# Column sums of an attention kernel: one fold by an accumulating DMA, the last half folded like the others

## The chip, the cores and the metric

The kernel runs on one core of a Trainium2 chip. The metric is the time of one execution on the device, in microseconds; the time of the kernel before is 1118.45 us, the median of three runs (1118.39 to 1118.84).

## The reference

Pooled attention, followed by a mixture of experts in which each token goes to one expert. All inputs are float32. The change lies in the attention, in the denominator of the softmax.

```python
# q, k, v: (8 batches, 8 heads, 1152 rows, 64)
q_pool = q.reshape(B, H, S // 2, 2, D).mean(axis=3)           # 576 queries
scores = (1.0 / np.sqrt(D)) * np.matmul(q_pool, k.transpose(0, 1, 3, 2))
scores = scores - np.max(scores, axis=-1, keepdims=True)
attn = np.exp(scores)
attn = attn / (np.sum(attn, axis=-1, keepdims=True) + 1e-09)
attn_out = np.matmul(attn, v)
x = attn_out.transpose(0, 2, 1, 3).reshape(4608, 512)         # tokens
# logits = x @ w_gate; each token to its argmax expert (of 8):
# out = gate_weight * (relu(x_e @ w1[e]) @ w2[e])
```

## The kernel before, in words

**Tiling.** The attention takes the eight batches one after the other, in each of them four pairs of heads (`hp` 0 to 3), in each pair two halves of the 576 pooled queries (`half` 0 and 1; `HQ` = 288 queries). One half of one pair is a unit; there are 64. A unit's scores stand in a tile `s` of 128 partitions x 9 chunks x 2 heads x 288, keys along the partitions. `scores` (from line 618 on) has TensorE form the products of a chunk into PSUM (`st`, line 640), VectorE take them into `s` with a running minimum (line 644), and ScalarE raise the whole to the exponential in place, two chunks at a time (line 675). `values` multiplies the exponentials with the values (`pa`, line 779).

**The column sums.** The denominators are sums over keys, that is over the nine chunks and the 128 partitions. `chunk_sum` makes them. GpSimd first folds the nine chunks of a unit to two: `fold` = chunks 0 to 2 plus chunks 3 to 5 (the first fold, 1728 numbers in a partition), plus chunks 6 to 8 (the second), then its third chunk onto its first (the third fold, 576 numbers); all three are on line 735. For a whole pair TensorE then multiplies both units' folded tiles with a matrix of ones, in four column strips of the array (`total`, line 725), and ScalarE or VectorE adds the result to `sm`. Two cases differ. The last pair of the last batch goes to TensorE unfolded (`whole`, line 718). And the second half of the last pair of every other batch is folded half way: GpSimd does the first fold alone (line 731), TensorE sums the three folded chunks and the three raw ones itself (line 718).

**What sets the order.** Every piece of work is recorded in a `Flow` with its engine, an estimate of its time, a key, the steps it needs and the tiles it holds; `emit` then walks through a plan in which each engine takes the ready step of the least key, and writes the instructions down in that order. So another piece of work in one place can move the instructions of every engine. On the chip each engine works through its own queue in order and waits by semaphores. Of `s` there are four buffers, of `fold` three. GpSimd also adds the two rows of each pooled query (`qp` from `qn`, line 529), and issues the scatters of the routing's lists (`lists`, line 960) of the batch before, six to a batch. SP issues the loads of `kp`, `qn` and `vn` (line 499).

**After the attention** the expert layers follow (lines 1363 and 1393), with weights `raw` loaded through SP and tokens gathered by GpSimd.

## Time and profile before

| what | value |
|---|---|
| median of three runs | 1118.45 us |
| the profiled execution: its time, its span | 1113.62 us, 1111.7 us |
| granted TensorE clock, mean | 0.999 of full speed |
| TensorE busy, share of the span | 1100.8 us, 99% |
| VectorE | 875.5 us, 79% |
| GpSimd | 854.2 us, 77% |
| ScalarE | 624.2 us, 56% |

The profile is of one execution; its span runs from the first to the last instruction, and its own time has a little around that. The attention ends at some 655 us of the span. PE is TensorE, DVE VectorE, ACT ScalarE, POOL GpSimd, SP the engine that issues most loads. A time in a timeline is counted from the span's start. The share of busy time is a mean over the whole program, so the views by stretch and by engine say more than the table. A matmul's record has a length of its own while the next one already runs, so the pace of TensorE is read from start to start; a float32 product stands in the profile as two records for each instruction of the order.

### The profile page before, as it was taken

To read this page: it belongs to the slowest core of one execution; us is meant where nothing else is said; L and a number is where in the kernel's file an instruction comes from. 1 tells how busy PE (TensorE), PEld (TensorE's weight loads), DVE (VectorE), ACT (ScalarE), POOL (GpSimd) and SP (SyncE) were. 2 spreads that over 40 slices of the span, in tenths; PEclk is the share of its full clock that TensorE was granted. 3 is DMA by queue.
4 is the path that set the end of the run, shared out by engine and by line. 5 is a ranking of instruction groups with operands and counts; after the bars stand their busy time and mean duration, and the time that the engine had idled before them with its cause. 6 is when DMAs were issued, how large, how long until landed. Compare 5 with 4: busy or idle time off the path is not lost.

```text
span 1111.7 us, 32995 instructions
## 1 busy us (share of the span) xinstructions
PE 1100.8 (99%) x13317; PEld 793.8 (71%) x13317; DVE 875.5 (79%) x2244; ACT 624.2 (56%) x835; POOL 854.2 (77%) x488
## 2 busy tenths in 40 slices
PE   9999999999999999999999999999999999999997
PEld 5555556565655565665665568999888989899896
DVE  7988988989989989989999959755555556677761
ACT  4656666566565666557655564444444444555561
POOL 3999999999999999999999943766666655555511
PEclk9999999999999999999999999999999999999999
DMA  9976747738648558558545069865555566677640
GB/s 159 167 120 111 128 76 123 129 66 125 115 73 139 97 85 141 94 89 146 81 84 107 3 227 212 244 180 176 176 169 167 184 195 191 194 248 252 224 159 30
DMA packets 387502, 158.06 MB, mean 142 GB/s; under 512 B 302694, under 2 KB 357762, under 8 KB 387342
## 3 DMA queue, kind: packets, MB, share of 16 engines
q1 hardware_dynamic: 376718, 134.91, 55.7%
q0 software_dynamic: 10464, 20.78, 5.8%
q8 instruction: 106, 1.74, 0.7%
q14 instruction: 54, 0.44, 0.2%
q10 hardware_dynamic: 160, 0.20, 0.1%
HBM read 135.02 MB, written 22.07 MB: 141 GB/s over the span
## 4 chain that ended last, share of the span: by engine, by line
PE 87%; issue 7%; POOL 4%; DVE 1%; DMA 1%; POOLq 0%; ACT 0%
PE st L640 24%; PE pa L779 24%; PE ph L1363 16%; PE py L1393 16%; PE st L725 3%; POOL fold L735 2%; PE st L718 1%; DVE s L644 1%; POOL xr L1092 1%; PE st L856 1%; PE st L665 1%; POOL out_dram L1402 1%; POOL xq L1092 1%; PE st L801 0%; DMA xr<-x_runs,ix 0%
## 5 line engine op out<-in xcount | busy, mean ns | idle before, releaser
L675 ACT ACTIVATE s<-s,bias 128x1152 f32<-128x1152 f32 (+1 forms) x320 | 346.7, 1149 | 172.5 <-DVE bias L671 172.4
L644 DVE TENSOR_SCALAR_CACHE_REDUCE s<-st 128x576 f32<-128x576 f32 x576 | 416.1, 746 | 30.3 <-PE st L640 28.1
L640 PE MATMUL st<-qT,kT 64*64 64x288 f32 x4608 | 363.6, 406 | 1.5 <-DVE s L644 0.9
L779 PE MATMUL pa<-s,vn 64*64 64x288 f32 x4608 | 358.5, 403 | 0.3 <-DVE xT L786 0.3
L640 PEld LDWEIGHTS st<-qT,kT 64*64 64x64 f32 x4608 | 167.4, 133 | 115.3 <-DVE s L644 22.4
L779 PEld LDWEIGHTS pa<-s,vn 64*64 64x64 f32 x4608 | 172.2, 133 | 98.4 <-DVE xT L786 3.5
L735 POOL TENSOR_TENSOR fold<-s 128x1728 f32<-128x1728 f32 x55 | 212.9, 3870 | 4.6 <-ACT s L675 4.4
L735 POOL TENSOR_TENSOR fold<-fold,s 128x1728 f32<-128x1728 f32 x55 | 213.4, 3879 | 0.5
L1363 PE MATMUL ph<-xh,w1h 128*128 128x248 f32 (+4 forms) x512 | 155.8, 304 | 0.6 <-DVE hl L1373 0.6
L1363 PE MATMUL ph<-xl,w1h 128*128 128x248 f32 (+4 forms) x512 | 154.6, 302 | 0.0
L1363 PE MATMUL ph<-xh,w1l 128*128 128x248 f32 (+4 forms) x512 | 154.6, 302 | 0.0
L1235 DVE TENSOR_TENSOR w2l<-raw,w2h 128x1024 fp32r<-128x1024 f32 x64 | 78.3, 1223 | 85.0 <-ACT w2h L1320 81.3
L1092 POOL DMA_INDIRECT xr<-x_runs,ix x76 | 96.8, 1274 | 51.8 <-issue 23.9
L1393 PE MATMUL py<-w2h,hh 128*128 128x512 f32 x328 | 128.1, 391 | 0.0
L1393 PE MATMUL py<-w2l,hh 128*128 128x512 f32 x328 | 127.8, 390 | 0.0
L1393 PE MATMUL py<-w2h,hl 128*128 128x512 f32 x328 | 127.8, 390 | 0.0
L1402 POOL DMA_INDIRECT out_dram<-y,rec x41 | 44.0, 1073 | 90.0 <-ACT y L1410 73.1
L1371 ACT ACTIVATE hh<-ph 128x372 fp32r<-128x372 f32 (+4 forms) x100 | 49.3, 493 | 106.5 <-PE ph L1363 106.4
L1363 PEld LDWEIGHTS ph<-xh,w1h 128*128 128x128 f32 x512 | 96.4, 188 | 3.4 <-DVE hl L1373 1.5
L1363 PEld LDWEIGHTS ph<-xl,w1h 128*128 128x128 f32 x512 | 96.5, 188 | 0.8
L1363 PEld LDWEIGHTS ph<-xh,w1l 128*128 128x128 f32 x512 | 96.5, 188 | 0.0
L1373 DVE SCALAR_TENSOR_TENSOR hl<-ph,hh 128x372 fp32r<-128x372 f32 (+4 forms) x100 | 55.6, 556 | 48.6 <-ACT hh L1371 48.5
(230 smaller groups left out, 1339.0 us busy)
## 6 DMA issues: line engine op xcount, KB each, us to landing
raw<-in_moe_w_dram SPq DMA_DIRECT2D x128, 512.0 KB
kp<-in_k_dram SPq DMA_DIRECT2D x124, 144.0 KB
vn<-in_v_dram SPq DMA_DIRECT2D x124, 144.0 KB
qn<-in_q_dram SPq DMA_DIRECT2D x120, 144.0 KB
x_runs<-row SPq DMA_DIRECT2D x96, 99.0 KB
xr<-x_runs,ix POOLq DMA_INDIRECT x76, 4.7
x_runs<-empty SPq DMA_DIRECT2D x4, 297.0 KB
xq<-x_runs,ix POOLq DMA_INDIRECT x52, 2.9
```

The lines of the kernel that those rows point to most:

```text
L640: nc.tensor.matmul(pt.t[to, h, :HQ], x.kT.t[up, c * P + i * D:c * P + (i + 1) * D], x.qT.t[up, cols], start=True, stop=True, tile_position ...
L644: nc.vector.tensor_scalar(s.t[:, c], pt.t[:, :, :HQ], -SCALE, None, op0=ALU.mult, op1=ALU.min, accum_out=mx.t[:, c:c + 1],)
L675: nc.scalar.activation(s.t[:, c0:c0 + n], s.t[:, c0:c0 + n], AF.Exp, bias=bias.t, scale=-1.0)
L735: add = lambda to, a, b: nc.gpsimd.tensor_tensor(to, a, b, ALU.add)
L779: mark.made = nc.tensor.matmul(pa.t[cs, i, :HQ], x.vn.t[up, h, c, :], s.t[up, c, h], start=c == 0, stop=c == NC - 1, tile_position=(up.sta ...
L1092: ins = nc.gpsimd.indirect_dma_start(out=x.xr[i // NQD].t[:, i % NQD, :], out_offset=None, in_=xg, in_offset=bass.IndirectOffsetOnAxis(ap= ...
L1235: (nc.gpsimd if eng == "POOL" else nc.vector).tensor_tensor(lo, raw, hi.bitcast(F32), ALU.subtract)
L1363: mark.made = nc.tensor.matmul(view()[:, i, :], a[:, c, fp], b[:, c, :n], start=c == 0 and k == 0, stop=c == NDC - 1 and k == 2)
L1371: a = f.add("ACT", act(nb * n) - 44, lambda home=home, apart=apart: nc.scalar.activation(home(0), apart(), AF.Relu), at - 20, done(p), [ph ...
L1373: d = f.add("DVE", dve(nb * n), lambda home=home, apart=apart: nc.vector.scalar_tensor_tensor(home(1), apart(), 0.0, home(0).bitcast(F32), ...
L1393: mark.made = nc.tensor.matmul(py.t, blocks(a)[:, c * x.nr + r], b[:, c % 2, :], start=c == 0 and k == 0, stop=c == NFC - 1 and k == 2)
L1402: ins = nc.gpsimd.indirect_dma_start(out=out, out_offset=bass.IndirectOffsetOnAxis(ap=x.re.t.bitcast(I32)[:, r, 0:1], axis=0), in_=y.t, in ...
```

## The change

The half-way case is gone: the second half of a batch's last pair is folded three times by GpSimd like the others, and `total` sums it. And in the first half of the first and the third pair (`hp` 0 and 2) of every batch but the last, the second fold is no longer an addition by GpSimd. GpSimd issues a DMA that reads chunks 6 to 8 of `s` and adds them to `fold` where it lies (`accum_op=ALU.add`, 884,736 B); the third fold waits for its landing. For the plan it stands as 1100 ns on GpSimd and 4700 ns on the DMA. `one` is false throughout, so the lines under it do nothing.

```diff
-        on_pe = by_units or not o.exact and hp == NHP - 1 and half == 1
+        on_pe = by_units
...
+        one = not o.exact and (False)
...
-        half_way = on_pe and not by_units
-        if half_way:
-            u = tile_of(o, "fold", [P, 3, 2, HQ], bufs=FOLD_BUFS, pool=o.rt)
-            p = f.add("POOL", pool(6 * HQ), lambda: nc.gpsimd.tensor_tensor(u.t, s.t[:, 0:3], s.t[:, 3:6], ALU.add),
-                      key, every(ready[:6]), [s, u])
-        elif not on_pe:
+        if not on_pe:
...
             p = f.add("POOL", pool(6 * HQ), lambda: add(u.t, s.t[:, 0:3], s.t[:, 3:6]), key, every(ready[:6]), [s, u])
-            p = f.add("POOL", pool(6 * HQ), lambda: add(u.t, u.t, s.t[:, 6:9]), key, done(p, *every(ready[6:])), [s, u])
+            if not o.exact and (half == 0 and b < B - 1 and hp % 2 == 0):
+                p = f.add("POOL", 1100, lambda: nc.gpsimd.dma_start(out=u.t, in_=s.t[:, 6:9], accum_op=ALU.add), key, done(p, *every(ready[6:])), [s, u])
+                p = f.add("DMA", 4700, lambda: None, key, done(p), [s, u], late=800)
+            else:
+                p = f.add("POOL", pool(6 * HQ), lambda: add(u.t, u.t, s.t[:, 6:9]), key, done(p, *every(ready[6:])), [s, u])
             p = f.add("POOL", pool(2 * HQ), lambda: add(u.t[:, 0], u.t[:, 0], u.t[:, 2]), key + R_FOLD3, done(p), [u])
...
-        if half_way:
-            parts.append(lambda: whole(ps, begin, [*(u.t[:, c] for c in range(3)), *(s.t[:, c] for c in range(6, NC))]))
-            needs, holds, ns = [*needs, *done(p), *every(ready[6:])], [*holds, s, u], ns + 485 * 3
-        elif on_pe:
+        if on_pe:
```

The change moves instructions. On GpSimd, around the last half of batch 3 and the first half of batch 4, the order before is this (the fold made of `s_4568` is the half-way one, the one of `s_4690` is batch 4's first):

```order
L735 TENSOR_TENSOR fold_4723<-fold_4723,s_4433 128x1728
L529 TENSOR_TENSOR qp_4840<-qn_4331 128x576
L731 TENSOR_TENSOR fold_4858<-s_4568 128x1728
L735 TENSOR_TENSOR fold_4723<-fold_4723 128x576
L735 TENSOR_TENSOR fold_4932<-s_4690 128x1728
L529 TENSOR_TENSOR qp_4990<-qn_4860 128x576
L735 TENSOR_TENSOR fold_4932<-fold_4932,s_4690 128x1728
L735 TENSOR_TENSOR fold_4932<-fold_4932 128x576
```

In the change, at the same place (`s_4539` is the last half, `s_4672` batch 4's first):

```order
L529 TENSOR_TENSOR qp_4816<-qn_4499 128x576
L732 TENSOR_TENSOR fold_4834<-s_4539 128x1728
L732 TENSOR_TENSOR fold_4697<-fold_4697 128x576
L732 TENSOR_TENSOR fold_4834<-fold_4834,s_4539 128x1728
L732 TENSOR_TENSOR fold_4963<-s_4672 128x1728
L732 TENSOR_TENSOR fold_4834<-fold_4834 128x576
L735 DMA fold_4963<-s_4672 128x1728
L529 TENSOR_TENSOR qp_5044<-qn_4838 128x576
L732 TENSOR_TENSOR fold_5066<-s_4796 128x1728
L732 TENSOR_TENSOR fold_5066<-fold_5066,s_4796 128x1728
L732 TENSOR_TENSOR fold_4963<-fold_4963 128x576
```

The last half has three folds now, the next unit's first fold among them, and its third fold is the fifth from its first on. Behind the issue of the transfer come the pooling of queries and two folds of the other half, and only then the third fold that needs its landing.

On GpSimd, in the third pair of batch 4, first half, where the lists' scatters of batch 3 stand, before:

```order
L735 TENSOR_TENSOR fold_5597<-s_5283 128x1728
L960 DMA lists<-re_5124,di_5441 42240x2
L735 TENSOR_TENSOR fold_5597<-fold_5597,s_5283 128x1728
L960 DMA lists<-re_5124,di_5441 42240x2
L735 TENSOR_TENSOR fold_5738<-s_5485 128x1728
L960 DMA lists<-re_5124,di_5441 42240x2
L735 TENSOR_TENSOR fold_5738<-fold_5738,s_5485 128x1728
L960 DMA lists<-re_5124,di_5441 42240x2
L735 TENSOR_TENSOR fold_5597<-fold_5597 128x576
```

In the change:

```order
L732 TENSOR_TENSOR fold_5558<-s_5252 128x1728
L960 DMA lists<-re_5112,di_5411 42240x2
L735 DMA fold_5558<-s_5252 128x1728
L529 TENSOR_TENSOR qp_5636<-qn_5381 128x576
L960 DMA lists<-re_5112,di_5411 42240x2
L732 TENSOR_TENSOR fold_5702<-s_5459 128x1728
L960 DMA lists<-re_5112,di_5411 42240x2
L732 TENSOR_TENSOR fold_5702<-fold_5702,s_5459 128x1728
L960 DMA lists<-re_5112,di_5411 42240x2
L732 TENSOR_TENSOR fold_5558<-fold_5558 128x576
```

The second fold `fold<-fold,s` of that half has become the DMA. The pooling of queries has moved behind it, and three scatters and two folds stand between the transfer's issue and the third fold.

On TensorE, the sum of batch 3's last pair, before:

```order
L640 MATMUL st_5040<-qT_4870,kT_4721 64x288 x4
L779 MATMUL pa_4947<-s_4568,vn_4222 64x288 x4
L725 MATMUL st_5057<-fold_4723,ones_73 32x288 x4
L718 MATMUL st_5057<-fold_4858,ones_73 32x288 x6
L718 MATMUL st_5057<-s_4568,ones_73 32x288 x6
L640 MATMUL st_5083<-qT_4870,kT_4721 64x288 x4
L779 MATMUL pa_5091<-s_4690,vn_4552 64x288 x4
```

In the change:

```order
L640 MATMUL st_5027<-qT_4836,kT_4705 64x288 x4
L640 MATMUL st_5037<-qT_4836,kT_4705 64x288 x4
L727 MATMUL st_5046<-fold_4697,ones_73 32x288 x4
L727 MATMUL st_5046<-fold_4834,ones_73 32x288 x4
L779 MATMUL pa_5061<-s_4672,vn_4532 64x288 x4
L665 MATMUL st_5074<-ident,top 64x64 x4
```

Of the sixteen matmuls of the sum eight are left, and those of the last half read its folded tile alone.

## Rows read from the trace of the kernel before

**Rows 1.** The page, part 1: busy us (share of the span) xinstructions.

```profile
PE 1100.8 (99%) x13317; PEld 793.8 (71%) x13317; DVE 875.5 (79%) x2244; ACT 624.2 (56%) x835; POOL 854.2 (77%) x488
```

**Rows 2.** Busy us by stretch (PE, PEld, DVE, ACT, POOL), clock, DMA share, GB/s.

```profile
400.00:500.00 100.00, 100.00 (x1672) 60.57 (x1668) 91.47 (x271) 62.15 (x78) 98.38 (x40) 1.00 0.62 102
```

**Rows 3.** GpSimd's timeline: start us, us, line, operation [idle before <-releaser].

```profile
366.73 3.86 POOL L735 TENSOR_TENSOR fold<-s 128x1728 f32<-128x1728 f32 x1 [0.71 <-ACT s L675]
...
411.12 3.90 POOL L731 TENSOR_TENSOR fold<-s 128x1728 f32<-128x1728 f32 x1
...
446.80 3.86 POOL L735 TENSOR_TENSOR fold<-s 128x1728 f32<-128x1728 f32 x1 [0.35 <-ACT s L675]
...
459.49 3.87 POOL L735 TENSOR_TENSOR fold<-s 128x1728 f32<-128x1728 f32 x1
...
464.47 3.87 POOL L735 TENSOR_TENSOR fold<-fold,s 128x1728 f32<-128x1728 f32 x1
...
480.80 3.89 POOL L735 TENSOR_TENSOR fold<-s 128x1728 f32<-128x1728 f32 x1
484.64 1.41 POOL L735 TENSOR_TENSOR fold<-fold 128x576 f32<-128x576 f32 x1
486.01 3.85 POOL L735 TENSOR_TENSOR fold<-fold,s 128x1728 f32<-128x1728 f32 x1
489.83 1.40 POOL L529 TENSOR_TENSOR qp<-qn 128x576 f32<-128x576 f32 x1
491.19 3.88 POOL L731 TENSOR_TENSOR fold<-s 128x1728 f32<-128x1728 f32 x1
```

**Rows 4.** The waits of GpSimd, 100 to 600 us: us in total, times, longest.

```profile
POOL fold L735 <- ACT s L675: 1.4, 3, 0.7
```

**Rows 5.** TensorE's timeline, batch 1, the sum of the third pair.

```profile
166.21 0.69 PE L725 MATMUL st<-fold,ones 128*32 128x288 f32 x8 [0.47 <-POOL fold L735]
```

**Rows 6.** TensorE's timeline in batch 5: the third pair's sum, then the last pair's.

```profile
486.46 1.18 PE L725 MATMUL st<-fold,ones 128*32 128x288 f32 x16
487.56 0.71 PE L779 MATMUL pa<-s,vn 64*64 64x288 f32 x8
...
504.45 0.69 PE L725 MATMUL st<-fold,ones 128*32 128x288 f32 x8
...
506.53 0.71 PE L640 MATMUL st<-qT,kT 64*64 64x288 f32 x8
```

**Rows 7.** DMA issues on GpSimd: lines 960 and 1056, the gathers' group, landing.

```profile
L960 POOL DMA_INDIRECT lists<-re,di x48: 915/922/1710, 130.7 to 684.6; - x48
...
DMA to landing us min/median/max: 3.4/5.1/6.1
...
L1056 POOL DMA_DIRECT2D li<-lists x13: 687/728/741, 695.7 to 930.7; - x13
...
L1092 POOL DMA_INDIRECT xr<-x_runs,ix x76 | 96.8, 1274 | 51.8 <-issue 23.9
```

**Rows 8.** Timelines, GpSimd and TensorE: the start, batch 0, batch 6.

```profile
22.50 3.89 POOL L735 TENSOR_TENSOR fold<-s 128x1728 f32<-128x1728 f32 x1 [2.25 <-ACT s L675]
...
31.94 1.41 POOL L529 TENSOR_TENSOR qp<-qn 128x576 f32<-128x576 f32 x1 [1.60 <-DMA qn<-in_q_dram]
...
91.62 3.87 POOL L731 TENSOR_TENSOR fold<-s 128x1728 f32<-128x1728 f32 x1
...
102.53 0.69 PE L725 MATMUL st<-fold,ones 128*32 128x288 f32 x8
...
584.52 0.69 PE L725 MATMUL st<-fold,ones 128*32 128x288 f32 x8
```

**Rows 9.** The page, part 3: packets, MB, share of 16 engines.

```profile
q0 software_dynamic: 10464, 20.78, 5.8%
```

**Rows 10.** VectorE's timeline, the second pair's queries turned.

```profile
38.66 0.47 DVE L542 STREAM_TRANSPOSE qT<-qp 128x288 f32<-128x288 f32 x1
```

**Rows 11.** DMA share in tenths, 40 slices, 420 to 500 us.

```profile
DMA  4599998775984799951750006949500006406999
```

More of the change, by code (lines that the diff above doesn't have):

```diff
@@ L736, in chunk_sum @@
             p = f.add("POOL", pool(6 * HQ), lambda: add(u.t, s.t[:, 0:3], s.t[:, 3:6]), key, every(ready[:6]), [s, u])
-            p = f.add("POOL", pool(6 * HQ), lambda: add(u.t, u.t, s.t[:, 6:9]), key, done(p, *every(ready[6:])), [s, u])
+            if not o.exact and (half == 0 and b < B - 1 and hp % 2 == 0):
[3 more added lines that the diff above has]
+                p = f.add("POOL", pool(6 * HQ), lambda: add(u.t, u.t, s.t[:, 6:9]), key, done(p, *every(ready[6:])), [s, u])
             p = f.add("POOL", pool(2 * HQ), lambda: add(u.t[:, 0], u.t[:, 0], u.t[:, 2]), key + R_FOLD3, done(p), [u])
+            if one:
+                p = f.add("POOL", pool(2 * HQ), lambda: add(u.t[:, 0], u.t[:, 0], u.t[:, 1]), key, done(p), [u])
             if half == 0:
@@ L748, in chunk_sum @@
             parts.append(lambda: total(ps, v, 0, True))
-            needs, holds, ns = done(q), [ps, v], 485
+            needs, holds, ns = done(q), [ps, v], 0 if one else 485
         begin = not parts
-        if half_way:
-            parts.append(lambda: whole(ps, begin, [*(u.t[:, c] for c in range(3)), *(s.t[:, c] for c in range(6, NC))]))
-            needs, holds, ns = [*needs, *done(p), *every(ready[6:])], [*holds, s, u], ns + 485 * 3
-        elif on_pe:
+        if on_pe:
             parts.append(lambda: whole(ps, begin, [s.t[:, c] for c in range(NC)]))
```

## The prediction, made before the changed kernel ran

> **What bounds the kernel now.** The page's busy line comes first: TensorE is busy for 99% of the span, GpSimd for 77% [rows 1]. A mean over stages with different limits says little, so next the busy time by stretch: in 100 us of the attention TensorE has 100.0 and GpSimd 98.4 [rows 2]. The reader is to see that two engines are full there, not one. Which of them sets the pace is read from GpSimd's timeline and its waits. From one of its waits for ScalarE to the next it works without a hole: it waits 0.71 us before the fold at 366.73 and 0.35 us before the one at 446.80 [rows 3], so one batch of its work takes 446.80 - 0.35 - 366.73 = 79.72 us. A batch itself takes 80.07 us (the half-way folds of two batches start at 411.12 and 491.19 [rows 3]). So TensorE sets the pace and GpSimd has 0.35 us to spare per batch; over 500 us it waits for work for 1.4 us in all [rows 4]. Early on it is the other way round: in batch 1 TensorE stands for 0.47 us in the middle of a sum, until a fold is done [rows 5]. A change that relieves one engine gains only until the other one holds it, and that is the whole question here.
>
> **TensorE's part.** The sum of a batch's last pair issues 32 records before (8 for the first half, 24 for the three half-summed and the three raw chunks), 16 after. The short form is there already: 486.46 to the next product at 487.56 is 1.10 us; the long one is 504.45 to 506.53, 2.08 us [rows 6]. Seven such sums save 0.98 us each, **6.9 us** in all, 80.07 - 0.98 = 79.09 us per batch. The order shows as many changes between the two ways of splitting the array as before, so nothing more comes off.
>
> **GpSimd's part, per batch.** From start to start [rows 3] a first fold takes 3.84 us (480.80 to 484.64), a third 1.37 (to 486.01), a second 3.82 (to 489.83), the pooling of a pair's queries 1.36 (to 491.19). Removed: two second folds, 7.64 us. Added: a second and a third fold for the batch's last half, 5.19 us, and two issues of a transfer. No accumulating transfer is in the trace. Below, its issue is bounded by the direct transfer of 128 rows, 0.73 us; above by the gathers, 1.27 us. The nearest indirect one, the scatter of the lists, takes 0.92 [rows 7], and with the gaps around it 1.14 us (459.49 to 464.47 less a fold [rows 3]). So an issue with its gap of 0.2 occupies 0.93 to 1.47 us; I take 1.05, between the direct one and the scatter, because it is direct but reads two places for each it writes. Net: -7.64 + 5.19 + 2.10 = -0.35 us, which makes **79.37 us** per batch (79.1 to 80.2). That is more than TensorE's 79.09: by these rows GpSimd takes over the pace.
>
> **Where the chain is tied.** The last half's sum now waits for five folds instead of one: its first fold, the third of the half before, its second, the next unit's first, its third, as the order shows, 3.84 + 1.37 + 3.82 + 3.84 + 1.37 = 14.24 us. Before, the sum of batch 0 stood 102.53 - 91.62 = 10.91 us behind that fold's start [rows 8], and waited for none of it. In batch 0 the transfer of the third pair lets GpSimd start it 3.82 - 1.05 = 2.77 us earlier, at 88.85, so the five end at 103.1. That of the first pair brings nothing: GpSimd then waits until 31.94 for queries anyway [rows 8]. From there six batches at 79.37 give 579.3 for the same sum in batch 6, which stood at 584.52 [rows 8]: 5.2 us earlier, and the sum itself is 0.98 shorter, **-6.2 us**. The last batch's work is as before.
>
> **What the transfers cost beside that.** (1) The first one is issued when the first fold of 22.50 is done, at 26.4, and flies while the next pair's queries come in, for which GpSimd already waits until 31.94 [rows 8]. Both source and target have to be read; 884,736 B at the mean rate of GpSimd's queue, 20.78 MB in 5.8% of 16 engines' 1111.7 us = 20.1 KB/us each, 322 in all [rows 9], are 2.75 us, twice that is 5.5. If its data flow from 27.5 on, the queries are held up for the 4.4 us until 31.94 at half their rate, 2.2 us; if only from 32 on, not at all. GpSimd's chain starts later by as much, TensorE's not, which wants these queries turned at 38.66 [rows 10]. I take **+1.0**, the middle. (2) Landing: the scatter, about 1 KB, lands 5.1 us after its issue [rows 7]. With 2.75 to 5.5 us of data the transfer lands after 7.9 to 10.6 us. In the first pair the order puts the queries' pooling and two folds between issue and third fold, 1.05 + 1.36 + 3.84 + 3.82 = 10.1 us of cover; in the third pair three scatters more, 13.5 us. So the wait at the first pair's third fold is 0 to 0.5 us; with 0.2 and six of them **+1.2**. The rule in the Trainium skill, "DMA: Bandwidth & Descriptors" (Anatomy of one DMA), gives an estimate of 2.0 us plus the bytes over 436 KB/us: 4.0 us, with no wait at all, and the sum would be 1.2 us lower. That the scatter takes 5.1 us for 1 KB speaks against it here. (3) Loads: a transfer can hold loads up by its 5.5 us. The cover is that the list of 500 us of GpSimd's waits names no load, ScalarE alone in more than the gaps of issues [rows 4]; without it the next query sum would wait that long. (4) The scores of a half are held until the landing instead of the second fold's end. They are overwritten four units later, 40 us, so that costs nothing.
>
> **Sum:** -6.2 + 1.0 + 1.2 = -4.0 us against the profiled execution's 1113.62 us (span 1111.7): 1109.6. The median of the runs shown, 1118.45, lies 4.83 above that execution, so the forecast is **1114.4 us**.
>
> **Rivals.**
> - *TensorE keeps the pace.* If the issue is at its low end and all landings are early, TensorE's 6.9 us and the 0.47 us that it waited [rows 5] come off: 1111.1. For it: the direct issue's 0.73 us. Against it: the five folds ahead of the last half's sum. Chance 0.10.
> - *Nothing is left.* An issue as long as a gather's, 1.27 plus a gap of 0.2, is 0.42 us more at 13 transfers (one in batch 0, two in each of six): -4.0 + 5.5 = +1.5, 1119.9, inside 0.2% (2.2 us, about what a measurement here can tell from no change). For it: the second read. Against: it is direct. Chance 0.17.
> - *Slower: the transfer lands after its cover.* Place: the third fold of the first pair's first half, which stands in GpSimd's queue; behind it are the next unit's first fold and everything else, and TensorE waits for that pair's sum. Each us of wait in six batches takes 6 us from the 5.2 that are left without landings; at 0.9 us nothing is left, at 1.25 it is slower by 0.2%, so it decides from a landing 11.3 us after the issue. With 2 us the time is 1118.45 - 5.2 + 12 = 1125.3. For it: load bursts fill the engines, 90% in many slices of a batch [rows 11], and a transfer that gets half of them needs 5.1 + 5.5 to 11 us. Against: the mean share is 62% [rows 2], and several slices in a row are idle [rows 11]. Chance 0.18.
> - *Slower: the issue itself is held up.* The longest scatter took 1.71 us against 0.92 [rows 7]; if each issue cost that and a gap, 1.9, 13 times 0.85 us more is +11.1: 1125.5. Against: 0.92 is median and nearly the least, beside a VectorE that is 91% busy [rows 2, 7]. Such a rule stands in the Trainium skill, "SBUF — State Buffer" (Who interferes with whom): GpSimd cannot write descriptors while VectorE runs in a mode that takes the port they share. By that rule the issue would stretch; these rows don't show it. Chance 0.04.
>
> **Numbers.** The forecast's own case has 0.51 and holds 1112 to 1116.5. Faster by over 0.2% are nearly all of it, the first rival and a little of the second: 0.58. Within 0.2%: the second and the edge of the late landing, 0.20. Slower: 0.22. The range goes from the first rival, 1111, to 1122, where the late landing means waits of 1.5 us; some 0.1 lies above it.
>
> **What would show it.** TensorE's records at the last pair's sum fall from 32 to 16, its busy time by some 6 us and a batch to 79.3 to 79.5 us. GpSimd's page line stands near 850 us, with 14 transfers of about 1.0 us, landing 8 to 10.6 us after issue; TensorE's waits for folds grow, at the batch's last sums. The forecast is wrong if a batch takes 79.1 us (TensorE), or 80 us and more with GpSimd waiting for a transfer ahead of third folds (late landing) or without such waits (dear issue), or if the first queries come more than 2 us later.

## The result, and the profile after

The changed kernel takes **1124.91 us** (median of seven runs, 1119.02 to 1129.78) where the kernel before takes 1118.45 (seven runs, 1117.55 to 1121.32): a ratio of 1.0052, with a 95% interval of 1.0031 to 1.0072. It is slower by half a per cent; forecast were 1114.4 us, faster by 0.36%. Timed again later, the same kernel came out at 1.0015 (0.999 to 1.004), 1.0004 (0.9995 to 1.0013) and 1.0003 (0.9993 to 1.0013). Here and below a ratio leaves out the few executions that ran in a slow state and the medians do not, so a ratio need not be that of two medians. So there are two questions: what eats the forecast gain everywhere, and what cost half a per cent more the first time.

The profiled execution took 1124.91 us, its span is 1123.3. The page's busy line and GpSimd's DMA queue, which answer to [rows 1, 9]:

```profile
PE 1101.2 (98%) x13205; PEld 810.6 (72%) x13205; DVE 878.6 (78%) x2244; ACT 622.8 (55%) x835; POOL 845.3 (75%) x502
...
q0 software_dynamic: 12480, 33.16, 12.1%
```

GpSimd is busy for 8.9 us less, but 5.3 of these lie in the gathers of the expert layers, which the change leaves alone (96.8 us before, 91.5 here). TensorE's busy time did not fall by the 6 us of the forecast in this execution. In a later pair of profiles on one chip (set 5 below) both come out as forecast: TensorE 1097.3 in place of 1102.5, GpSimd 851.1 in place of 855.2. The transfers, by their line (min/median/max ns of the issue on GpSimd):

```profile
L735 POOL DMA_DIRECT2D fold<-s x14: 839/978/1146, 27.7 to 550.2; - x14
```

The queue's 12.38 MB more are the 14 transfers; their data are 128 packets of 6912 B each, of 542 ns at the median and 623 at the mean. The first packet of a transfer begins 1.4 to 2.4 us after the issue (5.1 once), and the last one ends 6.7 to 9.2 us after it (11.4 the same once). GpSimd's waits from 100 to 570 us, beside [rows 4], name no landing of a transfer; the four largest are:

```profile
POOL lists L960 <- issue: 4.0, 24, 0.2
POOL fold L732 <- issue: 1.9, 3, 0.9
POOL fold L732 <- ACT s L675: 1.7, 2, 0.9
POOL qp L529 <- DMA qn<-in_q_dram: 1.2, 2, 0.8
```

Now the places where the two executions part. **The start.** GpSimd's timeline, beside [rows 8]:

```profile
23.50 3.88 POOL L732 TENSOR_TENSOR fold<-s 128x1728 f32<-128x1728 f32 x1 [2.04 <-ACT s L675]
27.72 1.15 POOL L735 DMA_DIRECT2D fold<-s  x1 [0.33 <-POOL fold L732]
38.58 1.42 POOL L529 TENSOR_TENSOR qp<-qn 128x576 f32<-128x576 f32 x1 [9.71 <-DMA qn<-in_q_dram]
```

The second pair's queries come at 38.58 us; before it was 31.94. What the DMA queues did from 30 to 34 us (packets, MB, share of 16 engines), in the kernel before, with its sizes of packets, and then in the changed one; the third fence is the changed one from 28 to 30 us, just ahead of the transfer's data, which flow from 30.1 to 36.1:

```profile
DMA packets 1757, 0.77 MB, mean 193 GB/s; under 512 B 1501, under 2 KB 1501, under 8 KB 1757
...
q1 hardware_dynamic: 1757, 0.77, 90.5%
```

```profile
q0 software_dynamic: 121, 0.84, 106.6%
q1 hardware_dynamic: 616, 0.08, 14.0%
```

```profile
q1 hardware_dynamic: 1894, 0.24, 76.1%
```

The loads do not flow at half their rate beside the transfer, they nearly stop: 0.08 MB in 4 us in place of 0.77. The two megabyte figures are not of the same loads, since 256 of before's packets are of over 2 KB and hold 0.59 of its 0.77 MB. Packets of one kind (under 512 B) tell it better: the changed kernel moves 1894 in the 2 us ahead of the transfer's data and 616 in 4 us beside them, a sixth of the rate. **The steady part and the rest.** Each batch begins with a spread of the tops (line 665). TensorE's rows at the first spread of batch 1 and of batch 7, and the first expert product, in the changed kernel:

```profile
94.42 0.29 PE L665 MATMUL st<-ident,top 64*64 64x64 f32 x8
...
574.38 0.29 PE L665 MATMUL st<-ident,top 64*64 64x64 f32 x8
...
669.34 0.44 PE L1363 MATMUL ph<-xh,w1h 128*128 128x372 f32 x1
```

and in the kernel before:

```profile
86.37 0.29 PE L665 MATMUL st<-ident,top 64*64 64x64 f32 x8
...
568.17 0.29 PE L665 MATMUL st<-ident,top 64*64 64x64 f32 x8
...
660.86 0.44 PE L1363 MATMUL ph<-xh,w1h 128*128 128x372 f32 x1
```

Batch 1 begins 8.05 us late, of which 1.01 stand at batch 0's first spread already (19.02 against 18.01), ahead of any transfer. The six batches take 479.96 us in place of 481.80, 79.99 each: 1.8 us won. The last batch takes 94.96 in place of 92.69: 2.3 lost. And in the expert layers, where nothing was changed, TensorE stands for 3.18 us, some 60 us behind the first expert product, because ScalarE takes up four instructions 1.1 to 2.2 us late. ScalarE's timeline there, then TensorE's row:

```profile
723.97 0.48 ACT L1371 ACTIVATE hh<-ph 128x372 fp32r<-128x372 f32 x1 [2.61 <-PE ph L1363]
724.35 1.05 ACT L1320 CAST w1h<-raw 128x1024 fp32r<-128x1024 f32 x1
727.62 0.57 ACT L1292 CAST xh<-px 128x496 fp32r<-128x496 f32 x1 [2.23 <-remote]
730.40 0.57 ACT L1292 CAST xh<-px 128x496 fp32r<-128x496 f32 x1 [2.21 <-PE py L1393]
732.06 0.69 ACT L1410 ACTIVATE y<-py,rec 128x512 f32<-128x512 f32 x1 [1.08 <-remote]
```

```profile
732.43 0.63 PE L1287 MATMUL px<-ident,xt 128*128 128x128 f32 x4 [3.18 <-DVE xt L1279]
```

The four differences, 8.05 - 1.84 + 2.27 + 3.18, make 11.7; the spans differ by 11.6. By the runs only 5.8 us (the ratio) to 6.5 (the medians) of that are the change's: the profiled execution of before, 1113.62 us, lies below all of its plain runs beside the result (1117.55 and more). That is why before was profiled again, below.

### The profile page after: what moved, and what is told of

It is laid out like the page before. It is cut to its first block, busy times and chain, and to the rows that moved or that the text cites. A ratio compares the mean times of both kernels' runs of the same rounds, so it can differ in the third digit from the quotient of the medians.

```text
span 1123.3 us, 32767 instructions
## 1 busy us (share of the span) xinstructions
PE 1101.2 (98%) x13205; PEld 810.6 (72%) x13205; DVE 878.6 (78%) x2244; ACT 622.8 (55%) x835; POOL 845.3 (75%) x502
## 4 chain that ended last, share of the span: by engine, by line
PE 87%; issue 5%; DVE 2%; POOL 2%; DMA 2%; SPq 1%; ACT 0%; another core or an unknown queue 0%; POOLq 0%; DVEq 0%; ACTq 0%
PE pa L779 23%; PE st L640 22%; PE py L1393 17%; PE ph L1363 17%; PE st L727 3%; DVE s L644 2%; POOL fold L732 1%; DMA qn<-in_q_dram 1%; SPq L499 1%; PE st L856 1%; PE st L665 1%; PE st L718 0%; PE st L801 0%; DMA raw<-in_moe_w_dram 0%; POOL out_dram L1402 0%
## 5 line engine op out<-in xcount | busy, mean ns | idle before, releaser
L640 PE MATMUL st<-qT,kT 64*64 64x288 f32 x4608 | 368.3, 406 | 4.8 <-DVE bias L671 2.4
L779 PE MATMUL pa<-s,vn 64*64 64x288 f32 x4608 | 365.9, 404 | 1.5 <-DVE xT L786 1.5
L640 PEld LDWEIGHTS st<-qT,kT 64*64 64x64 f32 x4608 | 177.5, 133 | 111.9 <-DVE s L644 25.4
L779 PEld LDWEIGHTS pa<-s,vn 64*64 64x64 f32 x4608 | 181.5, 133 | 94.0 <-DVE top L668 8.4
L732 POOL TENSOR_TENSOR fold<-s 128x1728 f32<-128x1728 f32 x62 | 241.8, 3900 | 6.5 <-ACT s L675 3.7
L732 POOL TENSOR_TENSOR fold<-fold,s 128x1728 f32<-128x1728 f32 x48 | 186.3, 3882 | 0.8
L1092 POOL DMA_INDIRECT xr<-x_runs,ix x76 | 91.5, 1204 | 53.2 <-issue 24.2
L1092 POOL DMA_INDIRECT xq<-x_runs,ix x52 | 60.1, 1155 | 48.5 <-PE py L1393 22.6
```

The lines of the kernel that those rows point to most:

```text
L640: nc.tensor.matmul(pt.t[to, h, :HQ], x.kT.t[up, c * P + i * D:c * P + (i + 1) * D], x.qT.t[up, cols], start=True, stop=True, tile_position ...
L732: add = lambda to, a, b: nc.gpsimd.tensor_tensor(to, a, b, ALU.add)
L779: mark.made = nc.tensor.matmul(pa.t[cs, i, :HQ], x.vn.t[up, h, c, :], s.t[up, c, h], start=c == 0, stop=c == NC - 1, tile_position=(up.sta ...
L1092: ins = nc.gpsimd.indirect_dma_start(out=x.xr[i // NQD].t[:, i % NQD, :], out_offset=None, in_=xg, in_offset=bass.IndirectOffsetOnAxis(ap= ...
```

## The experiments

There were eighteen runs of eleven kernels, in five sets; the runs of a set share a chip and the runs of before, and the sets follow here in order. In the first two sets before took 1119.87 and 1119.57 us, in the last three 1115.00, 1115.04 and 1115.54. Unless a table says otherwise, times are medians, and "batch" is the mean of batches 1 to 6, from first spread to first spread.

**The first transfer alone taken out** (`e1_not_first`), beside the change itself (`a_again`):

```diff
-            if not o.exact and (half == 0 and b < B - 1 and hp % 2 == 0):
+            if not o.exact and (half == 0 and b < B - 1 and hp % 2 == 0 and b + hp > 0):
```

> The changed kernel again, on the chip of the next three. Theory start (the first transfer holds up the second pair's queries, some 6 to 8 us of the time): again the pooling of these queries waits for their load until 36 us or later (31.94 before), batch 1 begins 6 us or more later than before (94.4 against 86.4 in the profile of the change), and a batch takes 80.0 us from then on. Rival (the start was an accident of one execution): queries pooled at 32 to 34 us. The expert layers' wait of 3.6 us on TensorE some 60 us after their begin, which the profile of the change shows and the one before does not: gone if it was an accident.

> The change without the very first transfer (batch 0, first pair); the second fold there is GpSimd's own again. Theory start: queries of the second pair pooled at 32 to 33 us, batch 1 begins at 87 to 89, and the time falls by 6 us or more against the changed kernel of the same call, to about 1118 (no different from before). Rival (the loss is spread over all batches, by waits for landings or contention): batch 1 begins earlier but the time falls by 2 us at most, and stays over 1121.

The change: 1125.07 us, ratio 1.0015 (0.999 to 1.004); queries of the second pair at 37.21, batches of 80.07, the wait in the expert layers again. Without the first transfer: 1122.10, ratio 1.0009 (0.9989 to 1.0029); the queries come at 32.92, batch 1 begins at 87.14, so the start is repaired. But batches took 80.42 and the expert layers' wait stayed, so the time fell by 3.0 us, not by the 6 or more of theory start.

**The other half of the change alone**: the transfers, with the half-way fold kept (`e2_half_way`), in the kernel before:

```diff
-            p = f.add("POOL", pool(6 * HQ), lambda: add(u.t, u.t, s.t[:, 6:9]), key, done(p, *every(ready[6:])), [s, u])
+            if not o.exact and (half == 0 and b < B - 1 and hp % 2 == 0):
+                p = f.add("POOL", 1100, lambda: nc.gpsimd.dma_start(out=u.t, in_=s.t[:, 6:9], accum_op=ALU.add), key, done(p, *every(ready[6:])), [s, u])
+                p = f.add("DMA", 4700, lambda: None, key, done(p), [s, u], late=800)
+            else:
+                p = f.add("POOL", pool(6 * HQ), lambda: add(u.t, u.t, s.t[:, 6:9]), key, done(p, *every(ready[6:])), [s, u])
```

> The kernel before with the 14 transfers alone: the last half is folded half way as before and TensorE sums the rest. GpSimd has 5.5 us per batch less to do and TensorE the same as before. Theory start: batch 1 begins some 6 us later than before, then 80.1 us per batch as before: about 1124. Rival contention (a transfer slows VectorE, TensorE or the loads while it flies): batches of 80.4 us and more, and 1127 or more. If GpSimd had set the pace before, batches would get shorter than 80.0.

1142.35 us, ratio 1.0137 (1.0098 to 1.0176). That is on the rival's side (1127 or more). GpSimd has time to spare now and TensorE gains nothing from it: batches of 80.4 to 81.0, and two of 91.5 and 90.5. The profiled execution is one of the longer ones, though (1148.28 us, of 1126.42 to 1153.42), so the two long batches need not stand in the others. In each of them TensorE stood once for a fold of GpSimd, 7.3 and 6.4 us, and after that its granted clock was at the lower level; why those folds came late was not followed, so the rival's contention is not shown. The first of the two, by stretch (PE, PEld, DVE, ACT, POOL, clock, DMA share, GB/s):

```profile
335.00:342.00 7.00, 3.88 (x64) 2.03 (x64) 3.55 (x13) 4.04 (x4) 6.81 (x4) 1.00 0.53 83
342.00:352.00 10.00, 5.62 (x48) 2.62 (x52) 1.54 (x4) 1.32 (x2) 10.00 (x5) 0.52 0.71 90
```

TensorE was busy for 3.88 of 7 us, and the next ten had 0.52 of full speed, that is 1.2 GHz.

**Less work for VectorE** (`e4_less_vector`), for the suspicion that VectorE, 92% busy, takes back what TensorE gains:

```diff
-        return f.add("DVE", 100 + dve(HQ), lambda: nc.vector.tensor_tensor(
-            xT.t[:, hp, to], xT.t[:, hp, to], pa.t[:, 1, :HQ], ALU.add), key + 20 + K_FREE + R_ADD, done(p, a), [pa, xT])
+        return a
```

> The change, with VectorE's addition of the second half of the values' product left out (line 786 of before, 0.45 us, eight times a batch; the outputs lack that half). Theory VectorE (TensorE's saved 1 us per batch is given back in waits for VectorE, which releases the score banks): batches of 79.0 to 79.4 us instead of 80.0, the time 4 to 6 us below the changed kernel. Rival GpSimd (its folds set the pace after the change): batches stay at 79.9 to 80.1 and the time changes by less than 2 us.

Tokens go to other experts then, so the total (1179.95 us) compares with nothing. The batches do: 80.10, 79.33, 79.88, 82.90, 80.26, 80.14. With some 2.6 us less for VectorE in 80, nothing was won: VectorE's load does not seem to hold the batches. The test is not a clean one, for in this kernel GpSimd also waited 7.3 us for TensorE's sums, which it does not in the change.

**Before, profiled again**, and **the new folds without transfers** (the condition of the transfers, `if not o.exact and (half == 0 ...)`, set to `False`):

> The kernel before, unchanged, profiled a second time. In its first profiled execution (1113.62 us, below all of its plain runs so far) the last batch took 92.7 us from its first spread of the tops to the first expert product, and TensorE never stood for over 0.8 us in the expert layers; in every profile of a kernel with transfers it is 94 to 95 us and a wait of 2.8 to 3.7 us stands 59.5 us behind the first expert product. Theory 1 (that execution was a lucky one, and these 5.8 us are not the change's): a last batch of 94 to 95 us, a wait of about 3 us at the same place, 1117 to 1121 us in all. Theory 2 (they come with the transfers): 92.7 us, no such wait, and a time near 1113.6. Both expect queries of the second pair at 32 us and batches of 80.0 to 80.4 us.

> The kernel before once more, as a second sample beside the other one: theory 1 expects a last batch of 94 to 95 us and the wait of about 3 us here too, at 1117 to 1121 us; theory 2 expects 92.7 us, no wait, 1113 to 1115 us. If the two samples differ, it is a matter of the execution, not of the kernel.

> The change without its transfers: the batch's last half is folded like the others, and all second folds stay GpSimd's. Theory (GpSimd has nothing to spare, so the transfers are what pays for the new folds): 79.7 us of GpSimd's work in a batch before plus a second and a third fold, 3.82 + 1.37 = 5.19, make 84.9 us per batch, six of them and the last half's longer wait 28 to 32 us slower than before, about 1149. Rival (GpSimd's order has slack that the waits do not show): 81 to 83 us per batch, 1125 to 1138.

Before: 1117.66 and 1118.28 us, queries at 33.4 and 33.6, batches of 80.52 and 80.53, a last batch of 93.6, and no wait at the place in the expert layers. So the first profile of before lies some 4 us under these (1.5 at the start, 1.3 in the batches, 0.9 in the last one). The start, with batch 1 at 86.37 us against 87.82 to 88.36 in the three later profiles, is in part luck; the batches and the last one are not luck alone, since before's profile in set 5 has them again (80.28 and 92.69). The wait was not left out by luck: theory 1 falls in that point. Against the first of these profiles, which is of another set, the change loses 6.6 us at the start, wins 3.2 in six batches, loses 1.4 in the last and 2.7 in the expert layers. The folds alone: 1145.14 us (two runs), 1.0225 (1.0202 to 1.0247), batches of 83.92, near the 84.9 of the theory. GpSimd was then busy for 98.7% of the stretch and TensorE for 96.7:

```profile
200.00:560.00 360.00, 348.15 (x5593) 224.03 (x5586) 315.58 (x951) 212.01 (x284) 355.23 (x145) 1.00 0.61 101
```

The transfers do pay for the new folds: 83.9 without them, about 80 with them. Neither half of the change, as run here, is any good alone.

**A third transfer per batch** (`e6_third_transfer`); the second edit alone, on the kernel without the first transfer, is `e9_later_third_folds` in the third set:

```diff
-            if not o.exact and (half == 0 and b < B - 1 and hp % 2 == 0):
+            if not o.exact and (b < B - 1 and b + hp > 0 and (half == 0 and hp % 2 == 0 or half == 1 and hp == NHP - 1)):
...
-                p = f.add("DMA", 4700, lambda: None, key, done(p), [s, u], late=800)
+                p = f.add("DMA", 7400, lambda: None, key, done(p), [s, u], late=800)
```

> The change without the transfer of the very first pair, and with a third transfer in each batch (six in all), for the second fold of the batch's last half; the planner is told 7.4 us for a transfer in place of 4.7, so that third folds stand further behind. GpSimd gets 3.82 - 1.0 = 2.8 us less work per batch, about 76.3. Theory A (in the steady part GpSimd, nearly full, eats TensorE's gain): batches of 79.0 to 79.4 us, against 80.0 to 80.4 with two transfers, so 4 to 6 us less than without the first transfer alone, some 1117. Theory B (VectorE, busy for 93 to 94%, hands TensorE its scores no sooner): batches still of 79.8 to 80.4 us, and the time 1121 to 1123. Theory C (a third transfer lands too late for the last half's sum or holds up loads): over 80.6 us, 1125 and more.

1152.79 us, 1.0293 (1.0275 to 1.0311), batches of 85.56: theory C in size, but not for its reason. GpSimd's timeline in batch 3:

```profile
272.71 1.30 POOL L735 DMA_DIRECT2D fold<-s  x1
276.21 1.40 POOL L732 TENSOR_TENSOR fold<-fold 128x576 f32<-128x576 f32 x1 [2.20 <-DMA fold<-s]
285.04 7.68 POOL L732 TENSOR_TENSOR fold<-s 128x1728 f32<-128x1728 f32 x2 [7.43 <-issue]
```

Only 2.20 us go to a landing. The 7.43 before the next first fold are a wait that no row names. Of the three `fold` buffers two are then held by halves whose transfers were issued 5.8 us apart, each for the 8 to 9 us to its landing and on to TensorE's sum. TensorE's timeline bears it out:

```profile
284.18 1.18 PE L727 MATMUL st<-fold,ones 128*32 128x288 f32 x16
```

GpSimd's next first fold starts at 285.04, within this sum, the only one from 262 us on that reads folded tiles and so gives buffers back. So the wait is for a buffer that TensorE's sum frees; a fourth buffer, which would test it, was not tried.

**Where ScalarE's instructions lie**, as a reason for the wait in the expert layers (kernels with transfers have 2 to 8 more ScalarE instructions ahead):

```diff
-    nc.scalar.activation(warm, ones[0:1, 0:1], AF.Exp)
+    for _ in range(9):
+        nc.scalar.activation(warm, ones[0:1, 0:1], AF.Exp)
```

> The kernel before with the first ScalarE instruction, an exponential of one element at 2.3 us, issued nine times instead of once; ScalarE has nothing else to do until 7.35 us, so this costs nothing by itself. In all kernels with transfers ScalarE reacts 1 to 3 us late to four instructions, 54 to 63 us behind the first expert product, and TensorE stands for 2.2 to 3.7 us there; they have 2 to 8 more ScalarE instructions ahead of the expert layers (639 to 645 records against 637), semaphore waits on the transfers. Theory 1 (the wait depends on where ScalarE's instructions lie, by their count, not on the transfers' data): 8 more instructions bring it into the kernel before, 2 to 4 us, about 1121. Theory 2 (it comes from the transfers in another way): no wait there, 1117 to 1119.

> The change without its very first transfer, and ScalarE's first instruction issued 21 times (20 more of 0.2 us, from 2.3 to 6.5 us, while ScalarE has nothing else to do until 7.35). Theory 1 (the count of ScalarE's instructions): the wait 59.5 us behind the first expert product goes or moves, and the time is 3 us below that kernel's, about 1119, equal to before. Theory 2: the wait stays, 1122.

> The change without its very first transfer, and the planner is told 7.4 us for a transfer instead of 4.7, which moves the third fold behind a transfer of the third pair by one fold (3.85 us) down GpSimd's order. With three transfers a batch, GpSimd stood 7.4 us in a batch for a fold buffer, of which there are three. Theory A (buffers: a transfer holds its fold buffer for 8 to 9 us, and what the third fold is put off holds it longer): batches no shorter than 80.4, rather 80.5 to 81.5, and a time of 1122 to 1126. Theory B (what is missing of the gain is lost in waits for landings): batches of 79.4 to 79.9, 1118 to 1120.

Before with 8 more: 1121.17 us against 1115.00. That is one execution. The wait did not appear, but the start lost 8 us (batch 0's first spread is at 26.81, at 18.01 and 18.99 in profiles of before), and that was the experiment's own doing. ScalarE also issues the first queries' load, which now stood behind the nine exponentials (ScalarE's queue, then TensorE):

```profile
2.25 2.07 ACT L335 ACTIVATE warm<-ones 1x1 f32<-1x1 f32 x9
4.12 0.86 ACTq L575 DMA_DIRECT2D s<-in_q_dram  x2
```

```profile
10.69 2.19 PE L605 MATMUL st<-ident,s 96*64 96x96 f32 x24 [5.72 <-DMA s<-in_q_dram]
```

The load is issued 2.9 us later than in the kernel before, TensorE stands for 5.72 us, and then has the lower clock for ten microseconds: 24 products take 2.19 us, not 1.21. By stretch:

```profile
5.00:8.00 3.00, 0.00 (x0) 0.00 (x0) 0.00 (x0) 0.00 (x0) 0.00 (x0) 1.00 1.07 266
...
11.00:14.00 3.00, 3.00 (x36) 2.76 (x32) 0.46 (x1) 0.00 (x0) 0.00 (x0) 0.50 1.40 141
```

The kernel without the first transfer and with 20 more (`range(21)`) pays 9 to 11 us at its start, against the same kernel without them (1120.43 us, 1.0044, 1.0026 to 1.0062), but its batches took 79.46 and it had no wait in the expert layers. Later third folds, with the start intact: **1111.97 us, 0.9973 (0.9965 to 0.9982)**, batches of 79.50, no wait: the first kernel that beats before. The batches are theory B's, the time lies under both theories' ranges. Since both kernels of this set, one with the old order of third folds, were free of the wait, the set itself came under suspicion, and the verdict on the count of instructions is void.

**The same kernels beside each other** (`e10_later_with_first` is the change with 7400 for 4700 and nothing else):

> The changed kernel once more, beside three kernels with transfers on one chip. The kernel with later third folds and no first transfer was 0.27% faster than before, on a chip where before took 1115.0; the one without the first transfer alone was 0.1% slower, on a chip where before took 1119.9. Theory P (the order of the third folds makes the difference): the change is 0.5% slower than before wherever it runs, some 5 us, with batches of 80 us, a last batch of 95 us and the wait of 3 us in the expert layers. Theory C (the chips differ): beside a before of 1115 the change loses its 6.6 us at the start and wins 3.6 in six batches of 79.5: 1117 to 1119, with no wait in the expert layers.

> The change without its first transfer, once more. Theory P: 5 us above the kernel with later third folds on the same chip, that is equal to before or slower by up to 0.3%, batches of 80.4 us. Theory C: within 1.5 us of that kernel, so 0.2 to 0.3% faster than before where before takes 1115, with batches of 79.5 us; where before takes 1119, both of them equal to before, with batches of 80.2 to 80.5 and the wait in the expert layers in both.

> The change without its first transfer and with later third folds, once more, on the chip of the other two. Theory P: 0.2 to 0.35% faster than before again, batches of 79.5 us, no wait in the expert layers. Theory C: as the kernel without the first transfer alone, whatever that is here.

> The change with all 14 transfers, and 7.4 us for a transfer in the planner's table in place of 4.7 (third folds later). Theory P: batches of 79.5 us and no wait in the expert layers, so only the start is lost, 5 to 7 us: 0.1 to 0.3% slower than before. Theory C: equal to the change on the same chip, within 1.5 us. Both expect the second pair's queries at 37 to 39 us.

> The change without its first transfer and with later third folds, a third time, to see whether its gain holds where the others lost. Where before takes 1113 to 1116 us: 0.25 to 0.35% faster again, batches of 79.5. Where before takes 1118 to 1121: if the late reactions of ScalarE in the expert layers come with any transfer there, a wait of 2 to 4 us stands 59.5 us behind the first expert product, batches take 79.9 to 80.4, and the time is equal to before within 0.2%; if the later third folds avoid them, no wait and 0.25 to 0.35% faster there too.

> The changed kernel, beside the other on the same chip. Its first transfer costs 5 to 7 us against the other kernel, wherever it runs: 0.4 to 0.6% above it. So equal to before where before takes 1113 to 1116, and 0.3 to 0.6% slower where before takes 1118 to 1121, with the wait in the expert layers.

> The kernel before, profiled on the same chip: batches of 80.07 us and 1113 to 1116 on a chip like the last one, of 80.3 to 80.5 and 1117 to 1121 on one like the first two; no wait of over 0.8 us 59.5 us behind the first expert product in either.

| kernel | set | us | ratio to before, 95% | queries | batch |
|---|---|---|---|---|---|
| the change | 4 | 1115.57 | 1.0004 (0.9995 to 1.0013) | 37.02 | 79.49 |
| the change | 5 | 1115.95 | 1.0003 (0.9993 to 1.0013) | 36.27 | 79.53 |
| the change, later third folds | 4 | 1116.79 | 1.0006 (0.9996 to 1.0016) | 36.70 | 79.38 |
| without the first transfer | 4 | 1111.19 | 0.9968 (0.9955 to 0.9981) | 31.79 | 79.66 |
| the same, later third folds | 4 | 1110.84 | 0.9967 (0.9956 to 0.9978) | 32.33 | 79.61 |
| the same, later third folds | 5 | 1111.79 | 0.9969 (0.9958 to 0.9980) | 31.68 | 79.47 |
| before | 5 | 1115.54 | | 33.93 | 80.28 |

Theory C holds in set 4, where the old and the new order of third folds differ by 0.35 us without the first transfer and by 1.2 with it. The order is not it; the first transfer is, worth 4.4 us with the old order (1115.57 against 1111.19) and 6.0 with the new (1116.79 against 1110.84). In set 5 it was 4.2 (1115.95 against 1111.79, with later third folds in the second alone), where 5 to 7 had been expected. That the second pair's queries land late there, and are not issued late, is seen from SP's issues of their load in set 4, without the first transfer and then with it:

```profile
24.05 3.59 SPq L499 DMA_DIRECT2D qn<-in_q_dram  x4
```

```profile
24.31 3.86 SPq L499 DMA_DIRECT2D qn<-in_q_dram  x4
```

None of the kernels of the last three sets has the wait in the expert layers, with or without transfers; all five with transfers that were profiled before, and whose tokens go to the same experts, have it (TensorE stands for 1.8 to 3.3 us). So by these profiles it comes with transfers and something else that differs between the sets, the chip or its condition. Sets 1 and 3 carry the same chip number, 2, so if the number names one chip, the chip alone is not it. What it is stays open: sets 4 and 5 did not show the wait, so nothing in them could take it away.

Set 5 gives the balance on one chip. TensorE's rows as above, of before and then of the change:

```profile
88.36 0.29 PE L665 MATMUL st<-ident,top 64*64 64x64 f32 x8
...
570.05 0.29 PE L665 MATMUL st<-ident,top 64*64 64x64 f32 x8
...
662.75 0.44 PE L1363 MATMUL ph<-xh,w1h 128*128 128x372 f32 x1
```

```profile
91.87 0.29 PE L665 MATMUL st<-ident,top 64*64 64x64 f32 x8
...
569.04 0.29 PE L665 MATMUL st<-ident,top 64*64 64x64 f32 x8
...
663.23 0.44 PE L1363 MATMUL ph<-xh,w1h 128*128 128x372 f32 x1
```

Start +3.5, six batches -4.5, last batch +1.5, the rest -0.2: +0.3 us in all, no change. The last batch, busy us by stretch in before and in the change, and in the change the waits of TensorE for folds (us in all, times, longest), of which before has none there:

```profile
570.06:662.75 92.69, 92.36 (x1486) 54.62 (x1478) 75.45 (x243) 54.97 (x73) 77.19 (x35) 1.00 0.40 95
```

```profile
569.04:663.24 94.20, 92.33 (x1470) 56.42 (x1462) 75.67 (x243) 54.99 (x73) 81.18 (x37) 1.00 0.41 98
```

```profile
PEld st L727 <- POOL fold L732: 2.1, 2, 1.3
...
PE st L727 <- POOL fold L732: 1.0, 2, 0.8
```

GpSimd has 4.0 us more to do in it. The second and third fold of batch 6's last half, 5.19 us by [rows 3], fall into the last batch, which has no transfer to pay for them. TensorE is idle for 1.9 us in it, 0.3 before; 1.0 of that is the wait for folds, and the rest was not followed.

## Why the prediction was wrong

**TensorE's part: right.** The last pair's sum is 16 records long in the result's profile, 1.11 us to the next product in place of 2.08 [rows 6]:

```profile
431.85 1.18 PE L727 MATMUL st<-fold,ones 128*32 128x288 f32 x16
432.96 0.71 PE L779 MATMUL pa<-s,vn 64*64 64x288 f32 x8
```

**GpSimd's part: right.** An issue takes 0.98 us (taken was 1.05 with its gap, from 0.93 to 1.47). In set 5 GpSimd's work of a batch, its waits and gaps left out, is 78.2 us in place of 78.5; the forecast's net was -0.35. So the rival of a dear issue falls, and that of an issue held up too: the longest took 1.15 us. The rule in the Trainium skill, "SBUF — State Buffer" (Who interferes with whom), did not show here; whether VectorE ran in such a mode, no row tells.

**The pace: right in the later sets, too short in the first.** Worked out were 79.37 us per batch, with GpSimd and TensorE almost level. Measured were 79.4 to 79.7 in the last three sets, in every kernel with two transfers a batch, and 79.99 in the result's own profile. A stretch of the latter, which answers to [rows 2]:

```profile
400.00:500.00 100.00, 99.82 (x1652) 67.82 (x1648) 91.66 (x271) 61.95 (x79) 98.37 (x43) 1.00 0.82 127
```

Both engines are as full as before. GpSimd's waits in this profile come to some 5.6 us beside the gaps of the scatters, in short pieces, against 2.3 in set 5. With both engines full, a short wait of one may be lost to the other as well; whether it is, and which of them begins it, these rows do not tell.

**Step (2), the landing: too dear.** 7.9 to 10.6 us were reckoned, 6.7 to 9.2 and once 11.4 measured, against a cover of 10.1 and 13.5; no wait for a landing, so the +1.2 is 0 and the rival built on it falls. The two parts of that sum were both off: the data took 5.1 to 7.3 us, not 2.75 to 5.5, and what stands ahead of them 1.4 to 2.4 (once 5.1), not the scatter's 5.1. Step (3) put the loads at nothing; from 100 us on GpSimd waited 1.2 us for queries in the result's profile, and not at all in those of the change in sets 4 and 5. The rule of the Trainium skill, "DMA: Bandwidth & Descriptors" (Anatomy of one DMA), gave 4.0 us. The trace of this accumulating transfer does not agree: its shortest landing is 6.7.

**Step (1), the first transfer: this is where the forecast failed.** I let the loads run "at half their rate" beside the transfer, and so put 2.2 us as the upper end and +1.0 into the sum. The rows show a sixth of the packets' rate, and 14.0% of the engines' time against the transfer's 106.6%, in 4 of the 6 us of its data. In set 4 the queries come 5.2 us later than without that transfer (37.02 against 31.79), nearly the whole 5.9 us of its data there, and the kernel is 4.4 us slower at its end. The sign that the prediction itself had named, queries more than 2 us later, is in the result's profile with 6.6 us (38.58 against 31.94). The bound was not one: it assumed equal shares of time for two queues whose packets are 6912 and here mostly 128 B long. A rule of the Trainium skill that I did not weigh speaks to that, "DMA: Bandwidth & Descriptors" (Queues, rings and completion order): each DMA engine goes round between its queues a packet at a time. By that rule the queue with the larger packets gets the larger share, and the trace agrees in that, with 0.84 MB against 0.08. One for one it is not, as the profile counts packets: 121 of the transfer's stand beside 616 of the loads', and in set 4 107 beside 134.

I also wrote that a late start of GpSimd's chain would leave TensorE's alone. It did not: in set 4 TensorE's batch 1 begins at 92.62 us with the transfer and at 86.16 without it.

**"The last batch's work is as before": wrong by 1.5 us.** Step "Where the chain is tied" followed the last half's new folds to TensorE's sum in batch 6, not to the next batch, where GpSimd does them.

Put right with the measured terms, the forecast's sum is -6.2 + 0.98 (the last sum's own saving lies inside the last batch and is counted there) + 4.4 + 1.5 = +0.7 us, and -3.7 without the first transfer. Measured in sets 4 and 5: +0.5 and +0.4, and -3.8 to -4.2. The 4.4 and the 1.5 come from these sets themselves, so this is no test of them; the balance of set 5 above has the same as +3.5, -4.5 and +1.5. What cost half a per cent more in the first timing, the expert layers' 3.2 us and 0.5 us per batch, was in no step and no rival. That part of the result is described here, not explained; in sets 4 and 5, which do not show it, the change is level with before.

The likeliest case had the mechanism of the steady batches right and one term, the first transfer's, more than four times too small. The rival on the other side ("lands after its cover") gave a time near the measured one, 1125.3, but for a reason that the trace refutes.

**The version to keep** is the change without its first transfer: 0.3% faster than before in three timings in the last three sets with later third folds, and once with the change's own order, while in the first set it only drew level (1.0009).

## What to carry to other kernels

When a large on-chip transfer takes work off a full engine, look first at what is being loaded while it flies. Where the program has no loads ahead, at its start above all, loads of small packets can nearly stop for as long as its data flow. Here the price was nearly that whole time (5.2 of 5.9 us), not half of it; leave the transfer out there. Follow each instruction that is added to an engine's queue to the place where that engine does it, past the end of the repeated part: the last round may inherit the cost and not the saving. And profile the kernel before more than once, for one profile can lie under all plain runs of its kernel: here it put 11.6 us between two executions where the runs showed some 6.

## What the runs showed of the hardware

An accumulating transfer from GpSimd of 884,736 B cost 0.98 us of issue and landed 6.7 to 9.2 us after it (once 11.4). Its 6912 B packets took 623 ns at the mean, 11.1 KB/us and engine, where the mean of that queue before was 20.1 [rows 9]. A load issued 2.9 us late put the first spread of the tops back by 8 us, since TensorE was first idle for 5.72 us and then had a granted clock of 0.5, that is 1.2 GHz, for ten microseconds; some 6 us of it were left at the end (1121.17 against 1115.00). A third transfer per batch, with later third folds, which alone did no harm (79.50), made it 5.0 us longer than before's in the same set (85.56 against 80.52), though it took work off GpSimd; what it used up was buffers, by the row of TensorE's sum at 284.18. And the same two programs stood 0.5% apart in one timing and could not be told apart in three others.
